# Attention on row halves of TensorE's array, with the softmax and gate factors applied to the value products, in a new order of steps

## The chip, the cores and the metric

One Trainium2 chip, one of its cores. The metric is the device time of one execution in microseconds (us); the kernel before took 457.18 us, the median of 3 runs (457.09 to 457.31).

## What is computed

Three layers, one after the other, for 2 sequences of 768 positions and 512 features: a retention layer, a feed-forward layer with a norm, and at last an attention layer with four heads (the experts) and a gate. The change is in the last one alone:

```python
logits = x @ w_gate                                  # 4 experts, the 2 best of each position count
topk = np.argpartition(-logits, K, axis=-1)[..., :K]
w = np.exp(sel - max); w /= w.sum(-1) + 1e-09        # sel: the logits of the 2 best
for e in range(E):
    q, k, v = x @ wq[e], x @ wk[e], x @ wv[e]        # 64 columns each
    scores = scale * (q @ k.transpose(0, 2, 1))
    scores = np.where(causal, -1000000000.0, scores)
    scores = scores - scores.max(-1, keepdims=True)
    a = np.exp(scores)
    a /= a.sum(-1, keepdims=True) + 1e-09
    ye = a @ v @ wo[e]
    out += mask[..., None] * w[:, :, kk:kk + 1] * ye  # mask: is e among the 2 best, kk: as which
```

## The kernel before, in words

TensorE works through its queue in an order that is written by hand; for the other engines, in this part, the framework decides the order. Until about 322 us it does the first two layers. What follows is the attention layer.

**Numbers in two parts.** Operands of the layer's products are kept as a high part, rounded to the matmul's fast 32-bit type (F32R), and a low part, the rest. A product then takes three passes (`PASSES`): high with high, low with high, high with low.

**Projections.** The positions stand in four blocks of 384 (two for each sequence). `qkv_steps` (L797) gives eight steps for a block: three value projections (`value`, L832, tile `pv`, 12 matmuls each), the gate (`gate`, L848, some 20 tiny VectorE instructions on a ranking, and an exponential), and four projections (`proj`, L809, tile `pj`, 12 matmuls of 384 columns each), two for the queries and two for the keys, each for a pair of heads: 64 rows for one head, 64 for the other. For the queries `qs` holds, for each head, the high part on that head's 64 partitions and the low part on the other 64. For the keys `kh` and `kl` hold the high and the low part on both halves of the partitions; GpSimd makes the second copy (L829).

**Rows.** The attention itself goes by row tiles (sequence, tile of 128 queries), in the order `ROWS`, four heads each: 48 items, numbered 0 to 47, four to a row tile. Row tile t looks at t + 1 blocks of 128 keys. `ORDER` (L62) names the steps of TensorE: `f` is the next step of the projections of blocks 1 to 3, and the others are of an item:

- `s` (`att_s`, L874): the scores of a head, two matmuls (`kh`, `kl`) over all 128 rows of the array for each piece of up to 512 columns. Up to 512 keys two heads share a PSUM tile `s` of two banks, above that a head has one for itself (two `big` tiles in all). VectorE masks the last block and takes the negative maximum, ScalarE takes the exponential into `att` and the sum into `ssum`.
- `c` (`att_c`, L911): VectorE adds a small number to the sum and takes the reciprocal, GpSimd multiplies all of `att` by it and by the gate's weight.
- `t` (`att_t`, L925): the 128x128 blocks of `att` are transposed by TensorE, up to four into a `mid` tile of one bank (four `mid` tiles in all, which projections, value products and outputs use too), and copied by ScalarE to `aT`.
- `v` (`att_av`, L936): the product with the values for a pair of heads, each on 64 columns of the array, into a `mid` tile `av`. After the second pair ScalarE and VectorE split it into `avs`.
- `o` (`att_o`, L954): the output projection of a row tile, six matmuls of 512 columns, a copy, and a store (SP's queue). The last row tile's is made in two halves.

## Time and profile before

| | |
|---|---|
| median of 3 runs | 457.18 us (457.09 to 457.31) |
| profiled execution, its own time | 457.37 us |
| its span | 455.6 us |
| PE, matmuls busy | 447.5 us (98%) |
| PEld, weight loads busy | 421.5 us (93%) |
| DVE busy | 331.9 us (73%) |
| ACT busy | 208.9 us (46%) |
| POOL busy | 83.2 us (18%) |

The profile is one execution. Times in its rows are us unless marked ns. PE is TensorE's matmuls, PEld its weight loads (which overlap PE), DVE VectorE, ACT ScalarE, POOL GpSimd, SP SyncE. L945 is line 945 of the kernel. Matmuls are pipelined and their recorded ends are modelled, so the time that one costs in a row of its kind is read from the chain of waits, which counts from start to start, and not from its recorded length. One fp32 matmul of the program stands as two in the trace (two passes), a fast one (F32R) and a transpose as one. A busy engine is not a bound by itself: what counts is which wait ends last at a place.

### The profile page before, as it was taken

How to read it: one execution, taken by the hardware profiler on the slowest of the kernel's cores; microseconds unless marked ns; L12 is line 12 of the kernel's file. 1: busy time of each engine (PE TensorE's matmuls, PEld its weight loads, DVE VectorE, ACT ScalarE, POOL GpSimd, SP SyncE). 2: the span in 40 equal slices, each digit the busy share in tenths (PEclk: the TensorE clock that was granted, in tenths of full speed). 3: DMA queues.
4: the chain of work that ended last, by engine and by line, in shares of the span. 5: the costliest groups of instructions: out<-in, count | busy, mean ns of one | idle time of the engine just before them, and what ended most of it. 6: DMA issues, size and time to landing. Idle time of an engine off the chain costs nothing.

```text
span 455.6 us, 9079 instructions
## 1 busy us (share of the span) xinstructions
PE 447.5 (98%) x3563; PEld 421.5 (93%) x3563; DVE 331.9 (73%) x698; ACT 208.9 (46%) x476; POOL 83.2 (18%) x132
## 2 busy tenths in 40 slices
PE   8799999999999999999999999999999999999997
PEld 4678889999999999999999999999999898999885
DVE  5688989859768768537789844655788886768763
ACT  3578865345533304113234522121366765648673
POOL 6647200000000000000000000000045445334440
PEclk9999999999999999999999999999999999999999
DMA  7997325214322122101223513130000000001011
GB/s 295 393 371 288 137 83 199 93 51 157 122 92 75 65 94 85 54 0 48 90 96 108 182 48 74 36 88 1 0 1 0 25 25 23 24 2 48 24 47 71
DMA packets 15226, 42.33 MB, mean 93 GB/s; under 512 B 2240, under 2 KB 5072, under 8 KB 15184
## 3 DMA queue, kind: packets, MB, share of 16 engines
q1 hardware_dynamic: 14896, 41.62, 26.7%
q8 instruction: 28, 0.46, 0.4%
q10 hardware_dynamic: 288, 0.13, 0.1%
q14 instruction: 14, 0.11, 0.1%
HBM read 35.43 MB, written 6.32 MB: 92 GB/s over the span
## 4 chain that ended last, share of the span: by engine, by line
PE 94%; DMA 3%; ACT 1%; issue 0%; POOL 0%; DVE 0%; SPq 0%
PE h L553 29%; PE y L589 27%; PE pj L815 7%; PE s L895 5%; PE av L945 5%; PE t L933 4%; PE pv L837 4%; PE o L966 4%; DMA early<-in_qkT 2%; PE po L431 2%; PE yf L611 2%; PE sc L367 2%; PE ps L412 1%; PE po L422 1%; DMA qk<-in_qkT 1%; PE va L471 1%
## 5 line engine op out<-in xcount | busy, mean ns | idle before, releaser
L553 PE MATMUL h<-xn,w 128*128 128x384 f32 x768 | 139.6, 336 | 0.0
L553 PEld LDWEIGHTS h<-xn,w 128*128 128x128 f32 x768 | 133.5, 188 | 2.2 <-DVE hs L575 0.6
L589 PE MATMUL y<-hs,w 128*128 128x384 f32 x552 | 99.7, 334 | 0.0
L589 PEld LDWEIGHTS y<-hs,w 128*128 128x128 f32 x552 | 96.1, 188 | 0.0
L572 ACT ACTIVATE hs<-h 128x384 fp32r<-128x384 f32 x50 | 24.5, 491 | 114.2 <-PE h L553 104.7
L829 POOL TENSOR_SCALAR kh<-kh 64x384 fp32r<-64x384 f32 x16 | 8.1, 507 | 295.4 <-ACT kh L826 293.4
L575 DVE SCALAR_TENSOR_TENSOR hs<-h,hs 128x384 fp32r<-128x384 f32 x50 | 27.7, 555 | 34.1 <-ACT hs L572 34.1
L923 POOL TENSOR_SCALAR att<-att,c,gw 128x128 f32<-128x128 f32 (+5 forms) x48 | 34.7, 730 | 46.0 <-DVE c L920 24.4
L597 DVE TENSOR_TENSOR xT<-xT,y 128x768 f32<-128x768 f32 x24 | 22.8, 952 | 27.3 <-PE y L589 27.3
L815 PE MATMUL pj<-x,wa 128*128 128x384 f32 x192 | 36.0, 340 | 0.0
L277 ACT CAST w<-top 128x512 fp32r<-128x512 f32 x32 | 19.8, 620 | 30.0 <-DVE top L269 30.0
L815 PEld LDWEIGHTS pj<-x,wa 128*128 128x128 f32 x192 | 33.1, 188 | 0.3 <-issue 0.2
L934 ACT COPY aT<-t 128x512 f32<-128x512 f32 (+3 forms) x64 | 26.4, 442 | 9.2 <-PE t L933 9.0
L933 PE MATMUL t<-ident,att 128*128 128x128 f32 x168 | 26.1, 275 | 0.0
L933 PEld LDWEIGHTS t<-ident,att 128*128 128x128 f32 x168 | 20.1, 140 | 3.1 <-issue 1.2
L895 PE MATMUL s<-kh,qs 128*128 128x384 f32 (+4 forms) x64 | 22.8, 362 | 0.0
L260 ACT ACTIVATE mag<-raw 128x512 f32<-128x512 f32 x31 | 20.4, 670 | 4.6 <-DVE w L288 2.1
L288 DVE TENSOR_TENSOR w<-top,mag 128x512 fp32r<-128x512 f32 x32 | 22.0, 688 | 0.3
L285 DVE TENSOR_TENSOR top<-top,w 128x512 f32<-128x512 f32 x32 | 21.9, 684 | 0.0
L282 DVE SCALAR_TENSOR_TENSOR mag<-raw,mag 128x512 f32<-128x512 uint32 x31 | 21.4, 689 | 0.7
L269 DVE SCALAR_TENSOR_TENSOR top<-raw,mag 128x512 int32<-128x512 int32 x31 | 21.4, 689 | 0.6
L945 PE MATMUL av<-aT,v 128*64 128x128 f32 x336 | 21.5, 277 | 0.0
(137 smaller groups left out, 701.0 us busy)
## 6 DMA issues: line engine op xcount, KB each, us to landing
raw<-in_w SPq DMA_DIRECT2D x31, 512.0 KB, 3.8
qk<-in_qkT SPq DMA_DIRECT2D x9, 512.0 KB, 5.5
kvn<-in_kv SPq DMA_DIRECT2D x9, 512.0 KB, 6.8
xd<-xT SPq DMA_DIRECT2D x4, 768.0 KB, 7.3
xr<-xd SPq DMA_DIRECT2D x8, 384.0 KB, 3.2
out<-os SPq DMA_DIRECT2D x11, 256.0 KB, 2.0
early<-in_qkT SPq DMA_DIRECT2D x3, 512.0 KB, 8.5
early<-in_kv SPq DMA_DIRECT2D x3, 512.0 KB, 6.6
```

What stands on the lines that cost most here:

```text
L288: nc.vector.tensor_tensor(t["w"][:, 1], t["top"], t["mag"], ALU.add)
L553: nc.tensor.matmul(ph[:, :TB], w[:, wi, k, :], xn[:, xi, k, :], start=(i == 0), stop=(i == 11))
L572: LAST.append([nc.scalar.activation(h[:, 0], ph[:, :TB], AF.Relu)])
L575: LAST[-1].append(nc.vector.scalar_tensor_tensor(h[:, 1], ph[:, :TB], 0.0, h[:, 0].bitcast(F32), ALU.max, ALU.subtract))
L589: nc.tensor.matmul(y[:, j, :TB], w[:, wi, e * P:(e + 1) * P], h[:, xi], start=(f == 0 and i == 0), stop=(f == GF - 1 and i == 2))
L597: nc.vector.tensor_tensor(xv, xv, y[:, :, :TB], ALU.add)
L815: nc.tensor.matmul(ps[:, :TB], w[:, wi, k, :], x2[:, xi, k, :], start=(i == 0), stop=(i == 11))
L895: nc.tensor.matmul(ps[:, c], q, kk[:, e, c * m:(c + 1) * m], start=(i == 0), stop=(i == 1))
L923: nc.gpsimd.tensor_scalar(a[:, :n], a[:, :n], c, gw, ALU.mult, ALU.mult)
L933: nc.tensor.transpose(pt[:, (j - j0) * P:(j - j0 + 1) * P], a[:, j * P:(j + 1) * P], ident)
L934: nc.scalar.copy(aT[:, j0 * P:j1 * P], pt[:, :(j1 - j0) * P])
L945: nc.tensor.matmul(pav[e2 * HD:(e2 + 1) * HD, pr * P:(pr + 1) * P], v[:, j, e * HD:(e + 1) * HD], row["aT"][e][:, j * P:(j + 1) * P], star ...
```

## The change

The scores of a pair of heads are computed together: each head's 64 rows of queries and keys are one half of the array's rows, in three passes (`PASSES`), a matmul for the one half and one for the other in turn, into different banks. (The product of low with low part, which the kernel before computed on the way, is left out.) The keys are no longer held twice, queries and keys are split for two heads at once. For more than 512 keys a score step takes both `big` tiles. A transpose of a block becomes two, of the upper and of the lower 64 queries, 64 columns each, into two `mid` tiles; blocks of two heads share them where they fit. The softmax's reciprocals and the gate's weights no longer scale `att`: GpSimd spreads their products over 64 columns a head (`wide`), two more blocks that are transposed with the last head's, and a new step `n` (`att_n`) multiplies the value product by them on its way out of PSUM, before the split. `c` and `n` are now steps of a row tile. `ORDER` is new.

```diff
--- before
+++ after
 ORDER = """
-    s0 s1 f f s2 s3 c0 s4 c1 c2 s5 c3 f s6 c4 s7 t0 t1 f c5 f t2 c6 f t3 s8 c7 s9 t4 c8 s10 v1 v3 t5 c9 c10 f t6
...
+    s4 s0 f f f s6 s2 c0 t5 f f f c4 t3 s8 s10 t1 f f t7 s16 t9 c8 f f v1 v3 t11 s18 t17 n0 f f f v9 v7 v5 v11 s12
...
-AT_BUFS = 8
+AT_BUFS = 5
+A_BUFS = 8
...
     def att_tiles(b):
         if b == 0:
-            kh, kl = (at.tile([P, E, S], F32R, tag=n, name=f"{n}{b}", bufs=1) for n in ("kh", "kl"))
+            KK[b] = at.tile([P, 2, 2, S], F32R, tag="k", name=f"k{b}", bufs=1)
         else:
-            kh, kl = (xnp.tile([P, E, S], F32R, tag="xn", name=f"{n}{b}") for n in ("kh", "kl"))
-        KK[b] = (kh, kl)
+            KK[b] = xnp.tile([P, 2, 2, S], F32R, tag="xn", name=f"k{b}")
...
-        qs = QS[blk] = at.tile([P, E, TB], F32R, tag="qs", name=f"qs{blk}", bufs=NBLK)
+        qs = QS[blk] = at.tile([P, 2, 2, TB], F32R, tag="qs", name=f"qs{blk}", bufs=NBLK)
...
                     nc.tensor.matmul(ps[:, :TB], w[:, wi, k, :], x2[:, xi, k, :], start=(i == 0), stop=(i == 11))
                     i += 1
-            for e2 in range(2):
-                e = 2 * (m % 2) + e2
-                r, o = ts(e2 * D, e2 * D + D), ts(D - e2 * D, 2 * D - e2 * D)
-                src = ps[r, :TB]
-                if m < 2:
-                    nc.scalar.mul(qs[r, e, :], src, HD ** -0.5)
-                    nc.vector.scalar_tensor_tensor(qs[o, e, :], src, HD ** -0.5, qs[r, e, :].bitcast(F32),
-                                                   ALU.mult, ALU.subtract)
-                else:
-                    nc.scalar.copy(kh[r, e, cs], src)
-                    nc.vector.tensor_tensor(kl[r, e, cs], src, kh[r, e, cs].bitcast(F32), ALU.subtract)
-                    for kk in (kh, kl):
-                        nc.gpsimd.tensor_scalar(kk[o, e, cs], kk[r, e, cs].bitcast(F32), 1.0, 1.0,
-                                                ALU.mult, ALU.mult)
+            pr, src = m % 2, ps[:, :TB]
+            if m < 2:
+                nc.scalar.mul(qs[:, 0, pr], src, HD ** -0.5)
+                nc.vector.scalar_tensor_tensor(qs[:, 1, pr], src, HD ** -0.5, qs[:, 0, pr].bitcast(F32),
+                                               ALU.mult, ALU.subtract)
+            else:
+                split(KK[b][:, 0, pr, cs], KK[b][:, 1, pr, cs], src)
...
-    def att_s(b, t, e):
-        kh, kl = KK[b]
-        qs = QS[2 * b + t // NTB]
-        q = qs[:, e, (t % NTB) * P:(t % NTB + 1) * P]
+    def att_s(b, t, pr):
+        k = KK[b]
+        q = QS[2 * b + t // NTB][:, :, pr, (t % NTB) * P:(t % NTB + 1) * P]
         n = (t + 1) * P
-        if e == 0:
+        if pr == 0:
             ROW[b, t] = dict(
                 negm=at.tile([P, E], F32, tag="negm", name=f"negm{b}{t}"),
                 ssum=at.tile([P, E], F32, tag="ssum", name=f"ssum{b}{t}"), a={}, aT={})
         row = ROW[b, t]
+        es = (2 * pr, 2 * pr + 1)
         negm, ssum = row["negm"], row["ssum"]
-        a = at.tile([P, S], F32, tag="att", name=f"att{b}{t}{e}", bufs=7)
-        row["a"][e] = a
-
-        pair = n <= 512
-        if not pair or e % 2 == 0:
-            row["s"] = ps_big(f"s{b}{t}{e}")
-        m = n if pair else n // 2
-        ps = row["s"][:, e % 2:e % 2 + 1, :m] if pair else row["s"][:, :, :m]
+        a = [at.tile([P, S], F32, tag="att", name=f"att{b}{t}{e}", bufs=A_BUFS) for e in es]
+        row["a"].update(zip(es, a))
+
+        short = n <= 512
+        m = n if short else n // 2
+        if short:
+            two = ps_big(f"s{b}{t}{pr}")
+            banks = [[two[:, i, :m]] for i in range(2)]
+        else:
+            ps = [ps_big(f"s{b}{t}{e}")[:, :, :m] for e in es]
+            banks = [[p[:, c] for c in range(2)] for p in ps]
         for c in range(n // m):
-            for i, kk in enumerate((kh, kl)):
-                nc.tensor.matmul(ps[:, c], q, kk[:, e, c * m:(c + 1) * m], start=(i == 0), stop=(i == 1))
-        if not pair:
-            nc.vector.copy_predicated(ps[:, 1, m - P:], tri, fill)
-            nc.vector.tensor_reduce(negm[:, e:e + 1], ps, AX.XY, ALU.max, negate=True)
-            nc.scalar.activation(a[:, :n].rearrange("p (c m) -> p c m", c=2), ps, AF.Exp, bias=negm[:, e:e + 1],
-                                 accum_out=ssum[:, e:e + 1])
-        elif e % 2 == 1:
-            two = row["s"]
+            for i, (ki, qi) in enumerate(PASSES):
+                for h in range(2):
+                    r = ts(h * D, (h + 1) * D)
+                    nc.tensor.matmul(banks[h][c], q[r, qi], k[r, ki, pr, c * m:(c + 1) * m], start=(i == 0),
+                                     stop=(i == 2))
+        if short:
             nc.vector.copy_predicated(two[:, :, n - P:n], tri[:, None, :].to_broadcast([P, 2, P]),
                                       fill[:, None, :].to_broadcast([P, 2, P]))
-            nc.vector.tensor_reduce(negm[:, e - 1:e + 1], two[:, :, :n], AX.X, ALU.max, negate=True)
-            for i in range(2):
-                f = e - 1 + i
-                nc.scalar.activation(row["a"][f][:, :n], two[:, i, :n], AF.Exp, bias=negm[:, f:f + 1],
-                                     accum_out=ssum[:, f:f + 1])
-
-    def att_c(b, t, e):
+            nc.vector.tensor_reduce(negm[:, es[0]:es[1] + 1], two[:, :, :n], AX.X, ALU.max, negate=True)
+            for i, e in enumerate(es):
+                nc.scalar.activation(a[i][:, :n], two[:, i, :n], AF.Exp, bias=negm[:, e:e + 1],
+                                     accum_out=ssum[:, e:e + 1])
+        else:
+            for i, e in enumerate(es):
+                nc.vector.copy_predicated(ps[i][:, 1, m - P:], tri, fill)
+                nc.vector.tensor_reduce(negm[:, e:e + 1], ps[i], AX.XY, ALU.max, negate=True)
+                nc.scalar.activation(a[i][:, :n].rearrange("p (c m) -> p c m", c=2), ps[i], AF.Exp,
+                                     bias=negm[:, e:e + 1], accum_out=ssum[:, e:e + 1])
+
+    def att_c(b, t):
         row = ROW[b, t]
-        n = (t + 1) * P
-        pair = n <= 512
-        if pair and e % 2 == 0:
+        c = at.tile([P, E], F32, tag="c", name=f"c{b}{t}", bufs=4)
+        nc.vector.tensor_scalar(c, row["ssum"], SUM_EPS, None, ALU.add)
+        nc.vector.reciprocal(c, c)
+        gw = GW[2 * b + t // NTB][:, t % NTB]
+        wide = row["wide"] = at.tile([P, E, HD], F32, tag="wide", name=f"wide{b}{t}")
+        nc.gpsimd.tensor_tensor(wide, c[:, :, None].to_broadcast([P, E, HD]),
+                                gw[:, :, None].to_broadcast([P, E, HD]), ALU.mult)
+
+    def half(r):
+        return ts(r * HD, (r + 1) * HD)
+
+    def alone(n, pr):
+        return n > 4 or n == 4 and pr == 1
+
+    def att_t(b, t, e):
+        row = ROW[b, t]
+        pr, n = e // 2, t + 1
+        if not alone(n, pr) and e % 2 == 0:
             return
-        for f in ((e - 1, e) if pair else (e,)):
-            c = at.tile([P, 1], F32, tag="c", name=f"c{b}{t}{f}", bufs=4)
-            nc.vector.tensor_scalar(c, row["ssum"][:, f:f + 1], SUM_EPS, None, ALU.add)
-            nc.vector.reciprocal(c, c)
-            a = row["a"][f]
-            gw = GW[2 * b + t // NTB][:, t % NTB, f:f + 1]
-            nc.gpsimd.tensor_scalar(a[:, :n], a[:, :n], c, gw, ALU.mult, ALU.mult)
-
-    def att_t(b, t, e):
-        row = ROW[b, t]
-        a = row["a"].pop(e)
-        aT = row["aT"][e] = at.tile([P, S], F32, tag="aT", name=f"aT{b}{t}{e}", bufs=AT_BUFS)
-        for j0 in range(0, t + 1, 4):
-            j1 = min(j0 + 4, t + 1)
-            pt = ps_mid(f"t{b}{t}{e}{j0}")
-            for j in range(j0, j1):
-                nc.tensor.transpose(pt[:, (j - j0) * P:(j - j0 + 1) * P], a[:, j * P:(j + 1) * P], ident)
-            nc.scalar.copy(aT[:, j0 * P:j1 * P], pt[:, :(j1 - j0) * P])
+        if pr not in row["aT"]:
+            row["aT"][pr] = at.tile([P, (2 * NC + 2) * P], F32, tag="aT", name=f"aT{b}{t}{pr}", bufs=AT_BUFS)
+        es = (e,) if alone(n, pr) else (e - 1, e)
+        from_ = [row["a"][x][:, j * P:(j + 1) * P] for x in es for j in range(n)]
+        if e == E - 1:
+            wide = row.pop("wide").rearrange("p (a e) d -> p a (e d)", a=2)
+            from_ += [wide[:, i] for i in range(2)]
+        j0 = es[0] % 2 * n
+        aT = row["aT"][pr][:, j0 * P:(j0 + len(from_)) * P].rearrange("p (j r q) -> p j r q", r=2, q=HD)
+        pt = [ps_mid(f"t{b}{t}{e}{r}")[:, :len(from_) * HD].rearrange("p (j q) -> p j q", q=HD) for r in range(2)]
+        for j, x in enumerate(from_):
+            for r in range(2):
+                nc.tensor.transpose(pt[r][:, j], x[half(r)], ident[half(r), half(r)])
+        for r in range(2):
+            nc.scalar.copy(aT[:, :, r], pt[r])
 
     def att_av(b, t, pr):
         row = ROW[b, t]
         v = VV[b]
-        if pr == 0:
+        if "pav" not in row:
             row["pav"] = ps_one(f"av{b}{t}")
-        pav = row["pav"]
         for j in range(t + 1):
             for e2 in range(2):
                 e = 2 * pr + e2
-                nc.tensor.matmul(pav[e2 * HD:(e2 + 1) * HD, pr * P:(pr + 1) * P], v[:, j, e * HD:(e + 1) * HD],
-                                 row["aT"][e][:, j * P:(j + 1) * P], start=(j == 0), stop=(j == t),
-                                 skip_group_check=True)
-        if pr == 1:
-            av = row["av"] = at.tile([P, 2, 2, P], F32R, tag="av", name=f"avs{b}{t}")
-            pv = pav[:, :2 * P].rearrange("p (a c) -> p a c", a=2)
-            nc.scalar.copy(av[:, 0], pv)
-            nc.vector.tensor_tensor(av[:, 1], pv, av[:, 0].bitcast(F32), ALU.subtract)
+                nc.tensor.matmul(row["pav"][half(e2), pr * P:(pr + 1) * P], v[:, j, e * HD:(e + 1) * HD],
+                                 row["aT"][pr][:, (e2 * (t + 1) + j) * P:(e2 * (t + 1) + j + 1) * P],
+                                 start=(j == 0), stop=(j == t), skip_group_check=True)
+
+    def att_n(b, t):
+
+        row = ROW[b, t]
+        n = 2 * (t + 1)
+        by = at.tile([P, 2, P], F32, tag="by", name=f"by{b}{t}")
+        flat = by.rearrange("p a c -> p (a c)")
+        nc.vector.tensor_tensor(flat, row["pav"][:, :2 * P], row["aT"][1][:, n * P:(n + 2) * P], ALU.mult)
+        av = row["av"] = at.tile([P, 2, 2, P], F32R, tag="av", name=f"avs{b}{t}")
+        nc.scalar.copy(av[:, 0], by)
+        nc.vector.tensor_tensor(av[:, 1], by, av[:, 0].bitcast(F32), ALU.subtract)
 
     def att_o(b, t):
         av = ROW.pop((b, t))["av"]
...
             continue
         if op[0] == "s":
-            att_s(b, t, e)
-        elif op[0] == "c":
-            att_c(b, t, e)
+            att_s(b, t, e // 2)
         elif op[0] == "t":
             att_t(b, t, e)
         elif op[0] == "v":
             att_av(b, t, e // 2)
         else:
-            att_o(b, t)
+            {"c": att_c, "n": att_n, "o": att_o}[op[0]](b, t)
```

What the new order moves, at the places that the prediction speaks of. `pj12` is a projection of block 1 (keys), `t003` the transposes of row tile (0,0) with head 3, `s020` scores of row tile (0,2), `av13` the value product of row tile (1,3), `o130` its output; `x12` counts instructions.

TensorE, early: the transposes of row tile (0,0) behind a projection, before.

```order
L815 MATMUL pj10_3695<-x2_1_3152,wa0_2905 128x384 x12
L933 MATMUL t0020_3713<-ident_129,att002_3589 128x128
L815 MATMUL pj12_3716<-x2_1_3152,wa1_2952 128x384 x12
L933 MATMUL t0030_3738<-ident_129,att003_3593 128x128
L895 MATMUL s020_3744<-kh0_3395,qs0_3398 128x384
```

The same place now:

```order
L812 MATMUL pj10_3671<-x2_1_3152,wa0_2905 128x384 x12
L812 MATMUL pj12_3686<-x2_1_3152,wa1_2952 128x384 x12
L943 MATMUL t0030_3707<-ident_129,att002_3615 128x64
L943 MATMUL t0031_3708<-ident_129,att002_3615 128x64
L943 MATMUL t0030_3707<-ident_129,att003_3616 128x64
L943 MATMUL t0031_3708<-ident_129,att003_3616 128x64
L943 MATMUL t0030_3707<-ident_129,wide00_3631 128x64
L943 MATMUL t0031_3708<-ident_129,wide00_3631 128x64
```

The blocks of both heads, and the two blocks of factors `wide` (each as two half blocks), stand behind both projections, and the scores `s020` behind them.

VectorE, ahead of those factors, now (`rank1`, `cmp1`, `mx1`, `gw1` are the gate of block 1, whose first instruction stands 12 rows above the first one here; `c00` the reciprocals of row tile (0,0)):

```order
L895 TENSOR_REDUCE negm00_3545<-s001_3617 128x2
L848 TENSOR_TENSOR rank1_3646<-rank1_3646,cmp1_3648 128x3x2
L845 TENSOR_TENSOR cmp1_3648<-v0_3396 128x3
L846 TENSOR_TENSOR rank1_3646<-rank1_3646,cmp1_3648 128x3
L847 TENSOR_TENSOR cmp1_3648<-v0_3396 128x3
L848 TENSOR_TENSOR rank1_3646<-rank1_3646,cmp1_3648 128x3
L854 SCALAR_TENSOR_TENSOR gw1_3663<-rank1_3646,gw1_3663 128x12
L855 TENSOR_REDUCE mx1_3661<-gw1_3663 128x3
L910 TENSOR_SCALAR c00_3628<-ssum00_3546 128x4
L910 TENSOR_SCALAR c01_3701<-ssum01_3531 128x4
L856 TENSOR_SCALAR mx1_3661<-mx1_3661 128x3
L911 RECIPROCAL c00_3628<-c00_3628 128x4
```

Before, the reciprocals `c00` of row tile (0,0) stood ahead of the first of that gate's instructions.

TensorE at the end, before:

```order
L933 MATMUL t1000_5132<-ident_129,att100_5011 128x128
L933 MATMUL t1010_5136<-ident_129,att101_5040 128x128
L966 MATMUL o140_5140<-wa3_3051,avs14_5079 128x512 x6
L933 MATMUL t1020_5158<-ident_129,att102_5054 128x128
L933 MATMUL t1030_5162<-ident_129,att103_5097 128x128
L945 MATMUL av10_5165<-aT100_5131,v1_3545 64x128
L945 MATMUL av10_5165<-aT101_5135,v1_3545 64x128
L945 MATMUL av10_5165<-aT102_5157,v1_3545 64x128
L945 MATMUL av10_5165<-aT103_5161,v1_3545 64x128
L966 MATMUL o130_5174<-wa3_3051,avs13_5128 128x512 x6
```

and now:

```order
L955 MATMUL av13_5231<-aT130_5066,v1_3527 64x128 x8
L955 MATMUL av13_5231<-aT131_5117,v1_3527 64x128 x8
L955 MATMUL av10_5248<-aT101_5218,v1_3527 64x128 x2
L955 MATMUL av10_5248<-aT100_5179,v1_3527 64x128 x2
L982 MATMUL o130_5264<-wa3_3051,avs13_5255 128x512 x6
L982 MATMUL o100_5274<-wa3_3051,avs10_5260 128x256 x6
```

Before, the value product `av13` stood ahead of these rows, with two transposes, an output projection and two more transposes between it and `av10`. Now the two value products follow one another, and `o130` follows them.

## Rows read from the trace of the kernel before

**Rows 1.** Page, part 1: busy time, share of the span, instructions.

```profile
PE 447.5 (98%) x3563; PEld 421.5 (93%) x3563; DVE 331.9 (73%) x698; ACT 208.9 (46%) x476; POOL 83.2 (18%) x132
```

**Rows 2.** Stretches: length, busy PE, PEld, DVE, ACT, POOL, granted clock, DMA share, GB/s.

```profile
322.00:452.50 130.50, 130.31 (x1050) 120.04 (x1048) 97.80 (x301) 82.36 (x223) 51.76 (x80) 1.00 0.06 21
407.50:452.50 45.00, 44.98 (x423) 39.22 (x421) 31.52 (x86) 30.96 (x85) 16.64 (x24) 1.00 0.10 36
```

**Rows 3.** Chain of waits from 280 us on: start, us, what.

```profile
by line: PE pj L815 19.2%; PE y L589 14.2%; PE s L895 11.8%; PE av L945 11.7%; PE t L933 10.5%; PE h L553 10.0%; PE pv L837 9.8%; PE o L966 9.6%; POOL kl L829 0.5%; DVE kl L827 0.3%; ACT kh L826 0.3%; ACT os L971 0.2%; issue 0.1%
...
326.87 8.38 PE pj L815 x48
...
347.51 0.59 PE av L945 x8
348.10 0.37 PE t L933 x2
...
361.60 0.79 PE s L895 x4
...
425.82 0.59 PE s L895 x4
...
441.20 2.33 PE av L945 x40
```

**Rows 4.** Chain of waits from 0 to 100 us, products on quadrants and column halves.

```profile
50.29 0.44 PE po L422 x16
...
51.75 0.47 PE ps L412 x16
...
57.22 0.60 PE po L422 x16
```

**Rows 5.** Timeline of the weight loads, 49.18 to 49.26 us.

```profile
49.18 0.21 PEld L367 LDWEIGHTS sc<-early 64*64 64x64 f32 x8 [0.62 <-DVE w L288]
```

**Rows 6.** Groups by line and shape, weight loads: busy us, mean ns, idle before.

```profile
L933 PEld LDWEIGHTS t<-ident,att 128*128 128x128 f32 x168 | 20.1, 140 | 3.1 <-issue 1.2
...
L895 PEld LDWEIGHTS s<-kl,qs 128*128 128x128 f32 x64 | 12.1, 190 | 0.5 <-POOL kl L829 0.4
...
L412 PEld LDWEIGHTS ps<-kvn,kd 128*64 128x64 f32 x128 | 4.8, 137 | 1.9 <-ACT kd L386 0.9 <-issue 0.8 <-POOL kd L392 0.2
```

**Rows 7.** Groups by line and shape on VectorE, 322 to 456 us.

```profile
L823 DVE SCALAR_TENSOR_TENSOR qs<-pj,qs 64x384 fp32r<-64x384 f32 x16 | 8.9, 555 | 4.5 <-ACT qs L822 4.2
...
L898 DVE TENSOR_REDUCE negm<-s 128x1 f32<-128x768 f32 x8 | 7.7, 957 | 0.2
L903 DVE COPY_PREDICATED s<-tri,fill 128x256 f32<-128x256 int32 x16 | 7.6, 473 | 2.6 <-PE s L895 2.4
...
L919 DVE TENSOR_SCALAR c<-ssum 128x1 f32<-128x1 f32 x48 | 6.9, 150 | 9.7 <-ACT att L908 5.1 <-ACT att L899 3.9 <-POOL att L923 0.3
...
L952 DVE TENSOR_TENSOR avs<-av,avs 128x256 fp32r<-128x256 f32 x12 | 5.0, 421 | 2.5 <-ACT avs L951 2.5
L897 DVE COPY_PREDICATED s<-tri,fill 128x128 f32<-128x128 int32 x16 | 4.9, 307 | 0.7 <-PE s L895 0.6
...
L905 DVE TENSOR_REDUCE negm<-s 128x2 f32<-128x512 f32 x4 | 2.8, 689 | 0.1
```

**Rows 8.** Groups by line on VectorE, 322 to 456 us, shapes together: the gate.

```profile
L858 DVE TENSOR_TENSOR rank<-rank,cmp 128x9 f32<-128x9 f32 (+2 forms) x12 | 2.9, 241 | 0.3
```

**Rows 9.** Groups by line and shape on ScalarE (322 to 456 us) and GpSimd (0 to 60 us).

```profile
L822 ACT ACTIVATE qs<-pj 64x384 fp32r<-64x384 f32 x16 | 7.7, 484 | 7.2 <-DVE qs L823 4.4 <-PE pj L815 2.7
...
L899 ACT ACTIVATE att<-s,negm 128x768 f32<-128x768 f32 x8 | 7.3, 908 | 1.8 <-DVE rank L856 1.0 <-DVE c L919 0.6 <-DVE negm L898 0.2
...
L951 ACT CAST avs<-av 128x256 fp32r<-128x256 f32 x12 | 4.5, 372 | 3.5 <-PE av L945 3.4
...
L447 POOL TENSOR_TENSOR old<-st,qpow 128x256 f32<-128x256 f32 x8 | 5.8, 721 | 5.2 <-DVE st L441 3.5 <-PE sc L367 1.6
```

**Rows 10.** List of waits: who for whom, us in total, times, longest.

```profile
PEld s L895 <- POOL kl L829: 0.4, 1, 0.4
```

More of the change, by code (lines that the diff above doesn't have):

```diff
@@ L62 @@
 ORDER = """
-    s0 s1 f f s2 s3 c0 s4 c1 c2 s5 c3 f s6 c4 s7 t0 t1 f c5 f t2 c6 f t3 s8 c7 s9 t4 c8 s10 v1 v3 t5 c9 c10 f t6
-    f s11 s12 t7 s13 f t8 c11 o3 f t9 s14 t10 c12 s15 v5 c13 v7 s16 c14 f t11 s17 c15 c16 t12 c17 s18 o7 v9 v11
-    f s19 t13 f t14 f f o11 c18 f t15 s20 c19 s21 t16 s22 c20 t17 v13 v15 s23 t18 s24 f o15 s25 c21 t19 c22 c23
-    s26 t20 c24 f f t21 c25 c26 s27 t22 f c27 f t23 f v17 v19 f f s28 s29 t24 c28 o19 c29 t25 s30 v21 v23 t26
-    s31 s32 t27 o23 t28 s33 c30 t29 s34 c31 c32 s35 v25 v27 c33 c34 c35 t30 s36 c36 o27 t31 s37 c37 t32 s38 v29
-    c38 v31 t33 s39 t34 s40 t35 s41 t36 o31 c39 c40 v33 c41 s42 t37 s43 t38 v35 c42 t39 s44 c43 o35 t40 s45 c44
-    t41 s46 v37 v39 c45 t42 c46 s47 t43 v41 v43 t44 t45 o39 c47 t46 t47 v45 v47 o43 o47
-"""
-AT_BUFS = 8
+    s4 s0 f f f s6 s2 c0 t5 f f f c4 t3 s8 s10 t1 f f t7 s16 t9 c8 f f v1 v3 t11 s18 t17 n0 f f f v9 v7 v5 v11 s12
+    s14 c16 c12 n8 f f f t13 f t14 s20 t15 t19 s22 v15 v13 t18 n4 o3 s24 f f f f t16 s26 f o11 t24 s28 t21 c20 f o7
+    f c24 n12 t25 s30 t26 v17 v19 t27 s32 n16 s34 v25 o15 t23 v27 n24 t28 t30 s36 c32 t29 v21 v23 o19 t36 s38 t35
+    v29 c28 n20 t31 o27 v31 c36 t38 t33 s40 t37 o23 t39 s42 v35 v33 v39 t41 v37 s44 c40 t42 t43 s46 n28 o31 n32 t45
+    n36 o35 o39 c44 t47 v41 v43 v47 v45 n40 n44 o43 o47
+"""
+AT_BUFS = 5
+A_BUFS = 8
 FRONT = """
@@ L872, in model @@
     ROW = {}
-    def att_s(b, t, e):
-        kh, kl = KK[b]
-        qs = QS[2 * b + t // NTB]
-        q = qs[:, e, (t % NTB) * P:(t % NTB + 1) * P]
+    def att_s(b, t, pr):
+        k = KK[b]
+        q = QS[2 * b + t // NTB][:, :, pr, (t % NTB) * P:(t % NTB + 1) * P]
         n = (t + 1) * P
-        if e == 0:
+        if pr == 0:
             ROW[b, t] = dict(
@@ L911, in att_c @@
-    def att_c(b, t, e):
-        row = ROW[b, t]
-        n = (t + 1) * P
-        pair = n <= 512
-        if pair and e % 2 == 0:
-            return
-        for f in ((e - 1, e) if pair else (e,)):
-            c = at.tile([P, 1], F32, tag="c", name=f"c{b}{t}{f}", bufs=4)
-            nc.vector.tensor_scalar(c, row["ssum"][:, f:f + 1], SUM_EPS, None, ALU.add)
-            nc.vector.reciprocal(c, c)
-            a = row["a"][f]
-            gw = GW[2 * b + t // NTB][:, t % NTB, f:f + 1]
-            nc.gpsimd.tensor_scalar(a[:, :n], a[:, :n], c, gw, ALU.mult, ALU.mult)
+            nc.vector.tensor_reduce(negm[:, es[0]:es[1] + 1], two[:, :, :n], AX.X, ALU.max, negate=True)
@@ L925, in att_t @@
+    def half(r):
+        return ts(r * HD, (r + 1) * HD)
+    def alone(n, pr):
+        return n > 4 or n == 4 and pr == 1
     def att_t(b, t, e):
         row = ROW[b, t]
-        a = row["a"].pop(e)
-        aT = row["aT"][e] = at.tile([P, S], F32, tag="aT", name=f"aT{b}{t}{e}", bufs=AT_BUFS)
-        for j0 in range(0, t + 1, 4):
-            j1 = min(j0 + 4, t + 1)
-            pt = ps_mid(f"t{b}{t}{e}{j0}")
-            for j in range(j0, j1):
-                nc.tensor.transpose(pt[:, (j - j0) * P:(j - j0 + 1) * P], a[:, j * P:(j + 1) * P], ident)
-            nc.scalar.copy(aT[:, j0 * P:j1 * P], pt[:, :(j1 - j0) * P])
+        pr, n = e // 2, t + 1
+        if not alone(n, pr) and e % 2 == 0:
+            return
+        if pr not in row["aT"]:
[13 more added lines that the diff above has]
+            nc.scalar.copy(aT[:, :, r], pt[r])
```

## The prediction

> **What bounds the kernel now.** I read the page's busy times first: TensorE's matmuls cover 447.5 of 455.6 us, 98% [rows 1]. In the part that the change touches, from 322 us on, PE is busy for 130.31 of 130.50 us at a granted clock of 1.00, VectorE for 97.8, ScalarE for 82.4, GpSimd for 51.8 [rows 2]. Then the chain of waits for the same part: nearly everything on it is PE, with the scores at 11.8%, the value products at 11.7% and the transposes at 10.5% of the 175.6 us of that view [rows 3]. Last the list of waits: of PE's own, the one that the change can take away is 0.4 us, on a GpSimd copy of the keys [rows 10]. So PE's queue is the clock of this part: a microsecond taken from a PE instruction is a microsecond won, and one taken from another engine is worth nothing unless PE waited for it.
>
> The profiled execution took 457.37 us, 0.19 more than the median of the runs shown (457.18). The sum is made against 457.37 and carried over to the median.
>
> **Scores.** Before, a head takes two matmuls of its n columns over the full array, so a pair of heads takes 4. Now it takes 3 passes, each as two matmuls on the two row halves (192 matmuls in 96 pairs, in place of 128). If the halves of a pair run at the same time, as the quadrants of the first part do (below), a pair costs what one full matmul did, and scores go to 3/4. The chain's 11.8% are 20.7 us, some 20 without the array's changes of shape that are booked there: **-5.0 us**.
>
> **Transposes.** Before: 168 blocks of 128 columns, 10.5% of 175.6 us [rows 3], 18.4 us or 0.11 a block. Now each block is two half blocks with 64 moving columns, on the upper and lower rows, and 24 blocks for the factors come in addition (2 for each of 12 row tiles): 192. The nearest row is the state product of the first part, 64 moving columns on column halves: 16 in 0.47 us, so 0.059 for two side by side; the state's read-out on quadrants runs 16 of 128 columns in 0.44 us, 0.11 for four [rows 4]. I take 0.059 a block: 11.3 us, **-7.1 us**.
>
> Do the weight loads of two halves overlap too? Eight loads of the quadrants begin and end within 0.21 us [rows 5], and one alone of 64 columns is recorded at 0.14 [rows 6], so loads of different quadrants do run together. And a load for a transpose, 128 columns, is recorded at 140 ns, one of 64 columns for the state at 137 [rows 6]: it should not be slower than the row that gave me 0.059. The Trainium skill, page "TensorE: Matmul & The Clock Gate", section "LDWEIGHTS (loading the stationary operand)", speaks against this change: a load costs its columns, not its rows, so a half block pays for a whole block's load, P/1.2 ns, 107 ns for 128 columns (an estimate by that page). If the two loads of a block queued at that price, 192 blocks would take 41 us and the time would come near 483 us. The trace has no load of 64 rows by 128 columns; what it has, loads of four quadrants inside 0.21 us, speaks for overlap; what such a queue would give by rows stands under rival 1.
>
> **Changes of the array's shape.** These cost something in the trace. Forty value products take 2.33 us and eight 0.59, so 0.054 each and 0.15 once for entering; two transposes right behind them take 0.37 in place of twice 0.11, again 0.15; four score matmuls behind them 0.79 in place of 0.59, 0.20 [rows 3]; the quadrants entered from the full array 0.60 in place of 0.44, 0.16 [rows 4]. By PE's order there were 26 such changes in this part. Now scores and transposes are on row halves, the projections and the output on the full array, the value products on column halves: 54 changes, 30 between full and row halves, 18 between row and column halves, 6 between full and column halves. 28 more at 0.15 to 0.20: **+4.9 us**. No row shows a change to 64 rows by 128 columns; if those 48 were free the term would be -3.4, at 0.30 each +11.0. I stay with the four rows, which agree.
>
> **From transposes to scores.** A score's weights load for 190 ns, a transpose's for 140 [rows 6], so 50 ns of it can no longer hide behind a half block of 59 ns. This happens 14 times: **+0.7 us**, at least 0.
>
> **Work that leaves or comes on other engines.** POOL (GpSimd) loses 48 scalings of the probabilities and 32 key copies, and gets 12 small products. VectorE loses 16 of 32 half-height subtractions of 0.56 (the other 16 take the full height) and 72 of 96 tiny sums and reciprocals of about 0.15 [rows 7], some 20 us, and gets 12 products of 128x256 at about the 0.42 of the subtraction of that size [rows 7], 5 us. ScalarE loses 16 half-height copies (0.48 each [rows 9], 7.7 us), and gets 24 more blocks to copy, some 3 us. All of it lies beside PE: in a part of some 126 us ScalarE has about 78 us of work, VectorE about 83. What it takes off the path is only the wait for the key copy: **-0.4 us**. In the last 45 us, where no projections are left, ScalarE was busy for 31.0 and VectorE for 31.5 [rows 2]; even there cover is left. The stores keep their number on SP; the last one leaves from the same step.
>
> **New waits on PE.** I went through PE's new order and compared at each step the work since the step it waits for. Three places come out.
> (a) The first factor tile. The transpose of heads 2 and 3 of row tile (0,0) now carries two blocks of factors, and everything behind it in PE's queue waits with it. The factors wait for the reciprocals, which VectorE has behind nearly the whole ranking of the second block, and the ranking waits for the third value projection. From the end of that: a ScalarE copy of 0.37 (as that of the products, of nearly the same width [rows 9]); twelve compares and sums of 0.24 or less [rows 8] and some five more, 3.3 in all; two score tiles with a mask of 0.47 and a maximum of 0.69 for the wider, about 0.4 for the narrower [rows 7], 2.05; four tiny ones, 0.6; a GpSimd product of 128x256, 0.72 [rows 9]: 7.1 us. PE has before it two score steps (0.7), one transpose (0.24), two projections (24 matmuls at 0.175 [rows 3], 4.2), three changes (0.5) and two blocks (0.1), 5.75. **+1.3 us**; 0 if the tiny instructions overlap, 2.5 if GpSimd is late.
> (b) The end. Before, the last but one row's products were followed by transposes and an output projection. Now four value steps stand in a row, and the projection behind them needs product, copy and subtraction: 0.42 + 0.37 + 0.42 [rows 7, 9] plus hops, against 0.44 us of value products left: **+0.9 us**.
> (c) Long rows now take both score tiles at once. The closest case is the pair behind the second half of row tile (1,5): the second tile is free after 2 x 0.31 + 2 x 0.957 + 0.908, 3.4 us [rows 7, 9], and PE has a transpose step, two value steps and a transpose step, 0.35 + 2.2 + 0.47, and two changes, 3.3. Elsewhere it has 4 to 6. With transposes that take two of the four small tiles at a time, I put **+0.5 us**, up to 4.
>
> **Sum:** -5.0 - 7.1 + 4.9 + 0.7 - 0.4 + 2.7 = -4.2 us. 457.37 - 4.2 = 453.2 for an execution like the profiled one; **453.0 us** against the median.
>
> **Rivals.**
> 1. *The halves take turns (slower)*, at their loads or in their streams. All overlap seen so far is of instructions that stream 128 columns in 0.11 us; a score streams 384 in the projection's 0.175, more than twice as fast, and two such streams into all 128 partitions are not in the trace. If only the scores queue, 192 matmuls cost 1.5 times the 20 us, +10.0 in place of -5.0: 468, a chance of 0.06. If only the transposes do, 192 x 0.118 = 22.7, +4.3 in place of -7.1: 464, 0.05. Both: 479, 0.03. The point from which it decides: 4.2 us over 192 blocks, 0.022 a block (0.081 in place of 0.059), or 0.044 on each of 96 score pairs. Against it: quadrants and column halves overlap perfectly [rows 4].
> 2. *PE waits where it saved.* ScalarE has to empty two tiles a transpose step, faster than before; if (c) is 4 us, (a) 2.5, and changes cost 0.25, 28 changes are 7.0 and the waits 7.4, and the sum is +2.7: 459.9. Against it: the loads of 62 to 66% worked out above.
> 3. *Changes to row halves are cheaper*, because two of the three shapes share their columns: down to free, 445 to 448. Against it: all four rows say 0.15 to 0.20.
>
> **How the numbers follow.** Forecast, 448.5 to 456.2: 0.62. Rival 1: 0.14, all slower. Rival 2, 456.2 to 460: 0.15, of which 0.07 lies within 0.2% and 0.08 slower. Rival 3: 0.09. A measurement of this kernel can tell 0.2%, 0.9 us, from no change. So faster 0.71, same 0.07, slower 0.22. The range from 447.5 to 460 takes in the forecast, rival 2 and the dearer part of rival 3; it leaves out rival 1 and the rest of 3, under 2 in 10.
>
> **What would show it.** In the new trace's chain, twelve half transposes should take 0.35 us, twelve score matmuls of 384 columns 1.05; each entry into another shape 0.15 to 0.20 more. The list of waits should show one wait of about 1 us of a transpose on GpSimd's factors and one of an output projection on VectorE's subtraction at the end. PE should still be over 95% busy from 322 us on. Twelve half transposes in 0.7 us, or twelve score matmuls in 2 us, would make the forecast wrong on rival 1's side; sums of PE waits over 6 us on rival 2's.

## The result and the profile after

| | before | after |
|---|---|---|
| median of 4 runs (lowest to highest), us | 457.22 (457.09 to 457.31) | 452.74 (452.42 to 452.81) |
| profiled execution, us | 457.37 | 452.42 |
| its span, us | 455.6 | 450.6 |
| granted clock | 1.00 | 1.00 |

After to before is 0.9901, with a 95% interval of 0.9884 to 0.9918: 4.5 us faster, where 4.2 had been forecast.

The page's busy times, to be held against [rows 1]:

```profile
PE 441.1 (98%) x3842; PEld 412.5 (92%) x3843; DVE 315.8 (70%) x622; ACT 202.8 (45%) x464; POOL 39.4 (9%) x64
```

PE lost 6.4 us and is still 98% busy. GpSimd's busy time halved, and PE's loads had waited for it only once, for 0.4 us [rows 10]. The stretches of the attention's part, as in [rows 2] (length, busy PE, PEld, DVE, ACT, POOL, clock, DMA share, GB/s):

```profile
322.00:447.50 125.50, 124.01 (x1328) 110.65 (x1326) 81.31 (x225) 76.43 (x211) 7.58 (x12) 1.00 0.07 24
407.50:447.50 40.00, 38.51 (x504) 31.72 (x500) 23.90 (x53) 25.08 (x73) 3.33 (x5) 1.00 0.15 54
```

PE is still the clock, at 99%; ScalarE's 76 us and VectorE's 81 are near the 78 and 83 of the prediction. Pieces of the chain of waits (start, us, what), for [rows 3]:

```profile
345.79 0.46 PE t L943 x8
...
351.87 0.52 PE t L943 x12
352.39 0.94 PE s L890 x12
353.32 0.36 PE t L943 x12
...
388.85 1.10 PE s L890 x12
...
403.60 2.33 PE av L955 x40
...
424.95 0.44 DVE by L965
...
440.68 1.92 PE av L955 x32
...
442.63 0.44 DVE by L965
...
443.14 0.41 ACT avs L967
...
443.60 3.08 PE o L982 x18
...
446.71 0.37 ACT os L987
```

Twelve half transposes, six blocks, take 0.36 (six whole ones took 0.66 by the old pace); entered from the full array, 0.52. Twelve score matmuls of 384 columns take 1.10: six pairs at 0.175, and 0.05 for following transposes. All that is not PE here are two products with the factors, one cast, and the last copy. The list of PE's waits has one entry:

```profile
PE o L982 <- ACT avs L967: 0.6, 1, 0.6
```

### The profile page after: what moved, and what is told of

The parts are those of the page before. It is cut to its first block, busy times and chain, and to the rows that moved or that the text cites. A ratio compares the mean times of both kernels' runs of the same rounds, so it can differ in the third digit from the quotient of the medians.

```text
span 450.6 us, 9348 instructions
## 1 busy us (share of the span) xinstructions
PE 441.1 (98%) x3842; PEld 412.5 (92%) x3843; DVE 315.8 (70%) x622; ACT 202.8 (45%) x464; POOL 39.4 (9%) x64
## 4 chain that ended last, share of the span: by engine, by line
PE 94%; DMA 3%; ACT 1%; issue 1%; POOL 0%; DVE 0%; SPq 0%; POOLq 0%; DVEq 0%; ACTq 0%
PE h L552 30%; PE y L588 28%; PE pj L812 8%; PE av L955 4%; PE o L982 4%; PE pv L827 4%; PE s L890 4%; PE t L943 3%; PE po L430 2%; DMA early<-in_qkT 2%; PE yf L610 2%; PE sc L366 1%; PE po L421 1%; DMA qk<-in_qkT 1%; PE va L470 1%; PE mean L479 1%
## 5 line engine op out<-in xcount | busy, mean ns | idle before, releaser
L914 POOL TENSOR_TENSOR wide<-c,gw 128x256 f32<-128x256 f32 x12 | 7.6, 638 | 383.0 <-DVE rank L841 296.6
L945 ACT COPY aT<-t 128x384 f32<-128x384 f32 (+5 forms) x68 | 27.8, 467 | 5.9 <-PE t L943 5.6
L897 ACT ACTIVATE att<-s,negm 128x256 f32<-128x256 f32 (+3 forms) x32 | 16.6, 529 | 9.5 <-DVE negm L895 4.9
L890 PE MATMUL s<-k,qs 64*128 64x384 f32 (+4 forms) x192 | 20.2, 336 | 0.0
L955 PEld LDWEIGHTS av<-aT,v 128*64 128x64 f32 x336 | 18.1, 137 | 1.9 <-issue 0.6
L982 PE MATMUL o<-wa,avs 128*128 128x512 f32 (+1 forms) x78 | 19.1, 387 | 0.6 <-ACT avs L967 0.6
```

The costliest lines, as they stand in the source:

```text
L890: nc.tensor.matmul(banks[h][c], q[r, qi], k[r, ki, pr, c * m:(c + 1) * m], start=(i == 0), stop=(i == 2))
L945: nc.scalar.copy(aT[:, :, r], pt[r])
L955: nc.tensor.matmul(row["pav"][half(e2), pr * P:(pr + 1) * P], v[:, j, e * HD:(e + 1) * HD], row["aT"][pr][:, (e2 * (t + 1) + j) * P:(e2 * ...
L982: nc.tensor.matmul(po[:, cs], av[:, xi, pr, :], wo[:, wi, pr, cs], start=(i == 0), stop=(i == 5))
```

## Experiments

Where no ratio is given, a time is of one execution, beside 457.1 of the kernel before on the same chip (457.2 for both heads on one half, 457.3 for the whole transposes).

**The halves in turns.** Does the gain come from two halves at work at once? The same matmuls in another order, first the scores', then the transposes'.

```diff
-        for c in range(n // m):
-            for i, (ki, qi) in enumerate(PASSES):
-                for h in range(2):
-                    r = ts(h * D, (h + 1) * D)
+        for h in range(2):
+            r = ts(h * D, (h + 1) * D)
+            for c in range(n // m):
+                for i, (ki, qi) in enumerate(PASSES):
```

> The changed kernel with the same 192 score matmuls in another order: all passes of the upper half, then all of the lower half. Theory (halves overlap, two side by side cost one): a step of 3 pairs becomes 5 single passes and one of 6 pairs becomes 11, since only the pass at the border still has a partner; 7.5 us of short steps x 2/3 and 7.7 us of long steps x 5/6 is +11.4 us, about 464. Rival (the halves take turns already, and the gain is the new order): no difference, 452.7. If not even the border overlaps, +15, 468.

```diff
-        for j, x in enumerate(from_):
-            for r in range(2):
+        for r in range(2):
+            for j, x in enumerate(from_):
```

> The changed kernel with the same 384 half transposes in another order: in each of the 34 transpose steps all upper halves first, then all lower halves. Theory (two half blocks run side by side in 0.059): 158 of 192 pairs lose their partner, +9.3 us, about 462. Rival (a half block is worth 0.030 by itself, so that two cost 0.059 in any order): no difference, 452.7. Rival (loads of the same half must queue behind its stream, 0.11 each): +25, 478.

Measured: 457.56 for the scores (+4.8) and 456.42 for the transposes (+3.7), less than half of what was expected. The timeline of PE in the run with the scores in turns (start, us, line, operation, count) shows why:

```profile
358.40 1.23 PE L890 MATMUL s<-k,qs 64*128 64x320 f32 x10
359.36 0.28 PE L943 MATMUL t<-ident,att 64*128 64x64 f32 x2
359.48 0.30 PE L890 MATMUL s<-k,qs 64*128 64x320 f32 x1
359.48 0.27 PE L943 MATMUL t<-ident,att 64*128 64x64 f32 x1
359.62 0.31 PE L890 MATMUL s<-k,qs 64*128 64x320 f32 x1
359.63 0.27 PE L943 MATMUL t<-ident,att 64*128 64x64 f32 x1
```

In the program all twelve score matmuls stand ahead of the transposes, six of each half in a row. Yet transposes start at 359.36, and two scores only after that, at 359.48 and 359.62: the two halves go through their own instructions, one ahead of the other. The expectation took the lower half to start with the upper one's last pass; by the starts it began with the third of six. So turns lose a few passes a step, not the partner, and these runs could not price the overlap. The next one could.

**Both heads on one half.** Here the work of both halves goes to one of them.

```diff
-                    r = ts(h * D, (h + 1) * D)
+                    r = ts(0, D)
...
-                nc.tensor.transpose(pt[r][:, j], x[half(r)], ident[half(r), half(r)])
+                nc.tensor.transpose(pt[r][:, j], x[half(0)], ident[half(0), half(0)])
```

> The changed kernel with all score matmuls and all half transposes on the upper row half: the second head's scores are computed from the first head's rows, and the lower half of each transposed block from its upper half. Left out: everything that the lower half computed. The order of instructions, their number and sizes stay. After the two runs in turns, which lost 4.8 and 3.7 us where 11.4 and 9.3 were expected, because each half goes through its own instructions and the lower half starts long before the upper one's are done: theory (two halves run side by side, whatever the order) loses the partner for good here, scores +15.2, transposes +11.3, together +26, about 479. Rival (a single half takes only part of the array's time, two in a row cost little more than one): +8 or less, the sum of the two runs in turns.

Measured: 479.09, +26.4. Pieces of its chain of waits, the same steps as in the chain above (320 columns here and there):

```profile
355.32 0.89 PE t L943 x12
356.21 1.81 PE s L890 x12
358.02 0.75 PE t L943 x12
```

0.94 became 1.81, 0.36 became 0.75: on one half each instruction pays in full, so two halves side by side cost what one does. By the starts of all matmuls, scores grew by 15.2 and transposes by 11.0 us. 0.75 for twelve is 0.063 a half block with its load. The Trainium skill, page "TensorE: Matmul & The Clock Gate", section "LDWEIGHTS (loading the stationary operand)", would have 0.107 for the load of its 128 columns alone (an estimate by that page): the trace disagrees with its 0.063 for load and transpose, and the measurement decides.

**What a change of shape costs.** One more matmul ahead of each score step, on the full array or on the upper half.

```diff
+        nc.tensor.matmul(banks[0][0][:, :P], q[:, 0], k[:, 0, pr, :P], start=True, stop=True)
```

> The changed kernel with one more matmul of 128 columns over the full array ahead of each of the 24 score steps (its result is overwritten by the step's first pass). It adds 40 changes of shape: 2 at each of the 19 score steps that follow a step on row halves, 1 at each of the 2 that follow value products. Theory (each change costs 0.14 to 0.20): against the same dummies on the upper row half (the other run) +5.6 to +8.0 us. Rival (changes between the full array and row halves are nearly free, what was seen is the change to and from column halves): +1 or less.

```diff
+        nc.tensor.matmul(banks[0][0][:, :P], q[:D, 0], k[:D, 0, pr, :P], start=True, stop=True)
```

> The control of the run with dummies on the full array: the same 24 matmuls of 128 columns, on the upper row half, so that no change of shape is added. Expected 24 x 0.11, +2.6 us over the changed kernel, about 455.3; less, down to +1, if the lower half's first pass runs beside the dummy.

Measured: 460.95 and 454.92. The difference of 6.0 us over 40 changes is 0.15 each, at the lower edge of what was expected; changes to and from row halves are not free. (This takes the added matmul to cost the same on the full array as on the upper half, where the 24 cost 2.2 us, 0.09 each.)

**Whole transposes.**

```diff
-        for j, x in enumerate(from_):
-            for r in range(2):
-                nc.tensor.transpose(pt[r][:, j], x[half(r)], ident[half(r), half(r)])
...
+            for j, x in enumerate(xs):
+                nc.tensor.transpose(pt[:, j * P:(j + 1) * P], x, ident)
```

> The changed kernel with the second part alone undone: 192 transposes of whole blocks of 128 columns in place of 384 half blocks, the same copies and the same order. Theory: 192 x (0.109 - 0.059) = +9.6 us, 57 changes of shape in place of 54 +0.5, no load of 190 ns behind a half block -0.7: +9.4, about 462. Rival (what the half blocks won is eaten by changes of shape around them): +3 or less.

Measured: 461.64, +8.9. A piece of its chain:

```profile
354.10 0.80 PE t L944 x6
```

Six whole blocks take 0.80, where six in halves, at the same place behind scores, take 0.36; the difference holds a change of shape. Of the 8.9 us, 1.0 lies behind the last matmul (4.9 us to the end of the span in place of 3.9; the section on the prediction shows why). Even so the second part alone is worth more than the whole gain.

**Factors on the probabilities again**, first right behind the exponentials, then one score step later.

```diff
+        for i, e in enumerate(es):
+            c = at.tile([P, 1], F32, tag="c", name=f"c{b}{t}{e}", bufs=4)
+            nc.vector.tensor_scalar(c, ssum[:, e:e + 1], SUM_EPS, None, ALU.add)
+            nc.vector.reciprocal(c, c)
+            gw = GW[2 * b + t // NTB][:, t % NTB, e:e + 1]
+            nc.gpsimd.tensor_scalar(a[i][:, :n], a[i][:, :n], c, gw, ALU.mult, ALU.mult)
...
-            from_ += [wide[:, i] for i in range(2)]
...
-        nc.vector.tensor_tensor(flat, row["pav"][:, :2 * P], row["aT"][1][:, n * P:(n + 2) * P], ALU.mult)
```

> The changed kernel with the third part alone undone: each head's probabilities are scaled on GpSimd right behind their exponential, as before the change (48 scalings), there are no factor blocks (24 pairs of half transposes less) and no product with the factors behind the value products. If the old work lay beside TensorE: -24 x 0.059 = -1.4 and about -0.4 at the end, 450.9. Rival (the third part is what makes the order possible: 72 tiny sums and reciprocals more on VectorE and a scaling of about 0.7 between exponential and transpose, so that transposes wait): slower, 455 or more.

In the text of the second kernel the same lines stand behind the next score step:

```diff
+            while late:
+                att_f(*late.pop(0))
+            late.append((b, t, e // 2))
```

> As the run with the factors on the probabilities, but the sums, reciprocals and scalings of a score step are issued behind the next score step's work, as the kernel before did, so that VectorE does not wait for the exponentials it has just asked for. If it was that wait (VectorE: 11 us for ScalarE's exponentials) that cost 3.4 us, the time falls to 451 to 453. If GpSimd's scalings and the way to them are late for the transposes whatever VectorE does, it stays at 455 or more.

Measured: 456.19 (ratio to the kernel before 0.9972, 0.9962 to 0.9981) and 456.16 (0.9977, 0.9968 to 0.9986). Both are 3.4 us slower than the changed kernel, though PE has 24 blocks less. (The last matmul ends 4.6 and 4.4 us later; the end behind it, for a reason given below, is 0.8 shorter.) The second run is no test of its question, though: in both traces all engines run the same instructions in the same order (on VectorE 682, on GpSimd 100), and from 322 us on each starts 0.12 to 0.21 us earlier in the second. The framework decides the order on these engines, and it came to the same one. So the second run repeats the first, and whether VectorE's wait for the exponentials makes the loss stays open. The longest of PE's waits in it:

```profile
PE o L974 <- ACT aT L940: 1.9, 2, 1.4
PE t L938 <- POOL att L913: 1.1, 3, 0.5
PE t L938 <- DVE avs L960: 0.8, 2, 0.4
```

GpSimd is named for 1.1 of some 4.5 us. One of the places, in the chain:

```profile
418.92 0.66 ACT att L903
...
419.61 0.20 ACT att L903
...
419.91 0.17 DVE c L910
...
420.10 0.17 DVE c L911
...
420.46 0.89 POOL att L913
...
421.39 0.52 PE t L938 x10
```

Exponential, sum, reciprocal, scaling, transpose: 1.6 us from the sum behind the exponential to the transpose. In the changed kernel only the transpose that carries the factors, one of a row tile, has such a way ahead of it. GpSimd, with 35 us of work in 128, isn't full; here it is late. The longest wait, 1.4 us of an output projection, names ScalarE's copy and not GpSimd. That the 3.4 us come from removing this part is shown; how much of them is GpSimd's way, and how much is ScalarE and VectorE, is not.

**Each kernel in the other's order.** First the changed kernel's steps in the old `ORDER` (where a step now serves two heads or a row tile, it stands where the even head's scores, the last head's factors and the last value products stood), then the kernel before in the new one. The two begin so:

```diff
-    s4 s0 f f f s6 s2 c0 t5 f f f c4 t3 s8 s10 t1
+    s0 f f s2 s4 c0 f s6 t1 f f f t3 c4 s8 v1 v3 n0
```

> The changed kernel's instructions in the order of the kernel before (pairs of heads where the head with the even number stood for the scores, the factors where the last head's stood, the product behind the last value products). 62 changes of shape in place of 54: +1.4 us by 0.17 each, and waits that the new order avoids, 0 to 3: 454 to 457. Rival (the gain is the order's): 457 or more. Rival (the new order brings nothing): 452.7.

```diff
-    s0 s1 f f s2 s3 c0 s4 c1 c2 s5 c3 f s6 c4 s7 t0 t1
+    s4 s5 s0 s1 c4 c5 f f f s6 s7 c0 c1 s2 s3 c6 c7 t4 t5
...
-AT_BUFS = 8
+AT_BUFS = 10
```

> The kernel before, all its instructions as they were, in the new order (two heads' scores together, the scalings behind the next scores, 10 transposed tiles in place of 8). Changes of shape 24 in place of 26, -0.3. Theory (the gain comes from the row halves, the new order only lets them keep it): 457 to 460. Rival (the order alone makes the gain): 453.

Measured, medians in us:

| | old order | new order |
|---|---|---|
| instructions before | 457.2 | 463.9 (ratio 1.0154, 1.0139 to 1.0170) |
| instructions after | 465.1 (1.0163, 1.0141 to 1.0185) | 452.7 (0.9901) |

Either half of the change alone loses 7 to 8 us. The new instructions in the old order came out far above the 454 to 457 of the theory, in the range of the rival (457 or more, the gain is the order's); but the order alone gains nothing either, it is dearer than both of its expectations (457 to 460, or 453). So neither makes the gain without the other. Of the loss in the first run (463.3 in its profiled execution, 10.9 above the changed kernel's), 1.2 us are 8 more changes of shape at 0.15; the list of PE's waits has much of the rest:

```profile
PE s L886 <- ACT att L899: 2.8, 3, 1.8
PE o L978 <- ACT avs L963: 2.4, 2, 1.9
PE av L951 <- ACT aT L941: 1.7, 3, 1.2
```

In the old order a score step that takes both score tiles stands too soon behind the last one. In the second run the list adds up to 3.7 us, the largest of it transposes that wait for VectorE; the rest of its 6.7 was not traced to a place. (Both orders were carried over by rule and not tuned to the other kernel; a better one may exist for either.)

**Another end.**

```diff
-    s46 n28 o31 n32 t45 n36 o35 o39 c44 t47 v41 v43 v47 v45 n40 n44 o43 o47
+    s46 n28 o31 n32 c44 o35 n36 t45 t47 v41 v43 n40 o39 v47 v45 n44 o43 o47
```

> The changed kernel with another order of its last 18 steps: two output projections ahead of the last transposes, one between the value products of the last two row tiles, so that no projection waits for its products. The changes of shape stay 54. Theory: the wait of 0.65 us of the output projection for ScalarE's cast goes, and the stores no longer stack, up to 0.4 more: -0.6 to -1.0, about 451.9. Rival (the end is set by the last store): no difference, 452.7.

Measured: 452.24 (452.00 to 453.06), ratio to the kernel before 0.9891 (0.9877 to 0.9906); the interval overlaps the changed kernel's, so this is no proven gain. The wait of the projection is gone, but the last matmuls end no sooner, since the transposes ahead of them now wait for ScalarE and there is one more change into value products:

```profile
443.92 3.02 PE o L978 x18
...
446.96 0.37 ACT os L983
```

They end at 446.94 in place of 446.68. What shrank is the time from there to the end of the span (450.2 and 450.6): 3.3 us in place of 3.9. This is not the stores' order, as the expectation had it; what it is stands under the end, below.

**Fewer changes.** Besides that end, steps are moved at five places, such as these:

```diff
-    f f f t13 f t14 s20
+    f f f f t13 t14 s20
...
-    t35 v29 c28 n20 t31 o27 v31
+    c28 t35 t31 v29 n20 v31 o27
```

> The changed kernel with the new tail and with steps moved at five more places, so that steps of the same shape stand together: 45 changes of shape in place of 54, two more places where scores follow transposes. By 0.15 to 0.17 a change -1.4 to -1.5, +0.1 for the two places, the tail -0.5, and new waits of 0 to 2 us, since the moved steps have less time: 450.9 if no wait comes up, 452.7 or more if TensorE waits where it saved.

Measured: 454.32 (ratio 0.9936, 0.9923 to 0.9948), slower than the changed kernel by 1.6. The dearest of its new waits, in the chain:

```profile
421.04 0.74 ACT att L903
...
421.83 0.88 ACT att L903 x2
422.71 0.97 ACT aT L945 x2
...
423.73 1.52 PE av L955 x22
```

The value step that now stands next to its transposes waits until ScalarE, which has three exponentials ahead, has emptied them. By the starts, PE takes 2.4 us more from the first value projection to the last matmul than in the changed kernel; with the 1.35 that nine changes at 0.15 give back, its waits have grown by some 3.7.

## Why the prediction was right

**Scores, -5.0.** The starts of the matmuls give 20.4 before and 15.2 after, less shape changes: -5.2. The run on one half shows the cause.

**Transposes, -7.1.** 18.3 and 11.3, so -7.0; the pace of 0.059 taken from the state's products [rows 4] was the right row. Rival 1 is refuted for both.

**Changes of shape, +4.9, and transposes to scores, +0.7.** 0.15 a change by experiment, so 28 are 4.2. The attention's part begins with these value projections, before and now:

```profile
322.55 4.32 PE pv L837 x36
322.27 4.32 PE pv L827 x36
```

From there to the end of the last matmul it is 129.9 us before and 124.4 now, 5.5 less. With -5.2 and -7.0 from scores and transposes, all that PE's time holds beside its instructions' pace, changes and waits together, grew by 6.7 us, against 7.9 forecast with the waits. Changes at 0.15, the 0.7, the waits below (0.9) and the wait for the key copy that is gone (-0.4) give 5.4 of it. The rest has no place; at 0.20 a change, as one of the prediction's rows has it, nothing would be left. Rival 3 is refuted.

**New waits, +2.7.** The term that was most off. (a) The first factor tile cost nothing, not 1.3: its eight half transposes follow the projection at 345.79 without a gap. The way from the third value projection to the reciprocals took 4.9 us, not 6.4, since VectorE's smallest instructions run into each other: these are recorded at 0.17 us each and start 0.08 and 0.12 apart.

```profile
340.94 0.17 DVE L846 TENSOR_TENSOR rank<-rank,cmp 128x9 f32<-128x9 f32 x1
341.02 0.17 DVE L852 TENSOR_TENSOR gw<-v,mx 128x12 f32<-128x12 f32 x1
341.14 0.17 DVE L847 TENSOR_TENSOR cmp<-v 128x9 f32<-128x9 f32 x1
```

The prediction had named this as its lower end. (b) came, 0.6 for 0.9, on ScalarE's cast and not on VectorE's subtraction: the projection's first passes need the high part alone. (c) One wait of 0.24 us for VectorE's product at 424.95 and one of 0.1, 0.3 in place of 0.5. Rival 2 did not come here; the runs with the old order and with fewer changes show that it could have.

**The step that was missing: the end.** "The stores keep their number on SP; the last one leaves from the same step" was put at nothing. It is right of the issues: on SP the last two begin 0.68 us ahead of the end of the last matmul, on ScalarE the last one 0.43 behind it, both before and now:

```profile
449.47 3.02 PE o L966 x18
451.81 0.81 SPq L972 DMA_DIRECT2D out<-os  x2
452.92 0.35 ACTq L972 DMA_DIRECT2D out<-os  x1
```

```profile
446.00 0.81 SPq L988 DMA_DIRECT2D out<-os  x2
447.11 0.35 ACTq L988 DMA_DIRECT2D out<-os  x1
```

Yet the end cost 0.85 us: before, the last matmuls were done 3.1 us ahead of the end of the span, now 3.9. What is new lies on the DMA queues (packets, MB, share; 452 to 456 us before, 446 to 451 now):

```profile
q1 hardware_dynamic: 288, 0.39, 27.4%
q10 hardware_dynamic: 144, 0.13, 9.5%
```

```profile
q1 hardware_dynamic: 288, 0.39, 22.2%
q10 hardware_dynamic: 144, 0.13, 8.1%
q14 instruction: 1, 0.01, 0.4%
```

One packet of 8 KB on an instruction queue runs from 448.16 to 448.47 us, among the packets of the last stores, and the last of these are held up behind it. In the 14 traces of this case, the last store's last packet ends 1.82 to 1.84 us behind the last matmul where no such packet falls among them (the kernel before, both orders exchanged, both runs with factors on the probabilities, the other end, fewer changes), and 2.52 to 2.55 where one does (the changed kernel, the runs in turns, on one half and with one more matmul; 3.54 in the run with whole transposes, behind one of 16 KB). So 0.7 of the 0.85 us come with this packet. The prediction counted the program's own stores alone; why the packet comes when it does, no run here settles.

So PE's part is 5.5 us shorter (-5.2 - 7.0 + 6.7), its last matmul ends 5.8 us earlier (0.3 lie ahead of the attention's part, where nothing was changed), the span is 5.0 shorter. A wait that did not come and an end that was not seen cancelled in part; some of the near hit is luck.

**The factors, put at nothing for the path.** "All of it lies beside PE" is right of the busy time and says little of the worth: without this part the same order loses 3.4 us. Scaling on GpSimd then lies between exponential and transpose, which accounts for a part of that; the rest is open. The forecast's sum is unharmed, because the waits were looked for in the new order with the factors already moved.

**Two slips that change nothing.** Rival 1 has a score stream "more than twice as fast" as the quadrants' 128 columns in 0.11 us; 384 in 0.175 is 1.9 times. Rival 2's terms add up to +2.6, not +2.7.

## What to carry to other kernels

Two matmuls of 64 rows on different row halves, loads included, cost what one does, so a product with 64 rows to contract, and a transpose cut in two, can halve; each change of the array's shape takes 0.15 us back. A step that serves twice as much at once needs an order that gives it time: here the new instructions in the old order lost 8 us, and saving nine changes of shape lost more in waits than it won. What lies off the path by busy time may still be what an order lives on: ask how long the way through it is, not only how full the engine. And look whether an edit reached the trace before reading its time: where a framework orders an engine, lines that were moved in the text may run where they ran before.

## What the runs showed that was not expected

The two halves do not keep the program's order between them. With six passes of one half ahead of six of the other, the second half began about three passes in, and transposes of the next step began up to 0.26 us ahead of scores that stand before them (359.36 and 359.62 in the timeline above). The Trainium skill, page "TensorE: Matmul & The Clock Gate", section "The mechanism", says that matmuls start in program order; in these traces that holds within a half and not across the two.
